# Three small re-orderings in a fused adaLN + linear attention + GEGLU kernel: one residual addition, one product's bank, two modulations

## The chip, the cores and the metric

One core of a Trainium2 chip runs the whole program. The time is device microseconds of one execution; the kernel before stands at 788.48 us, the median of three runs.

## What is computed

With x of 2048 tokens by 1024 columns, all inputs in bf16:

```
sa, ca, ga, sb, cb, gb = (silu(c) @ w_mod) cut into six rows of 1024
h = layernorm(x) * (1 + ca) + sa
x = x + ga * (linear_attention(h; wqkv, 32 heads) @ wo)
h = layernorm(x) * (1 + cb) + sb
x = x + gb * ((gelu(h @ w_gate) * (h @ w_up)) @ w_down)        # 3584 inner columns
```

## The kernel before

The tokens are 16 tiles of 128 ("chunks" c0 to c15), in four groups of 512. The work goes through four stages: layernorm and the K/Q projections; the attention sums and the output product; the feed-forward's gate and up products; the down product.

**Program order and queues.** Every instruction is recorded with `sch.op(engine, ...)` or `sch.dma(...)` together with the bytes and PSUM banks that it reads and writes. A tracker turns those into semaphore waits. Each engine (TensorE is PE, VectorE is DVE, ScalarE is ACT, GpSimd is POOL, SyncE is SP and issues nearly all transfers) then runs its list strictly in order. For the stretch from the last K tiles to the second feed-forward unit, `Sched.reorder` rewrites the lists of DVE, ACT and POOL: a planner with a cost per instruction and a due time worked back from the end picks the ready instruction that is due first. PE's and SP's lists stay as recorded.

**From attention to the feed-forward.** `wo_chunk(c)` makes 16 matmuls (L1266) of a chunk's attention output into two banks. Then one DVE instruction, `x1` (L1274), adds the result to the residual x in SBUF (`XALL`) and leaves the row sums for the next layernorm. From these come the row statistics (POOL L666 to L681, ACT L676), the normalised chunk (ACT L662) and a transposing transfer into `H2` (L705). Then the modulation by `1 + cb` and `sb` is done in place, one instruction for each of eight column blocks: on DVE (`mod2`, L726) or on ACT (`mod2_act`, L755). The chunks c2 to c13 go through a loop whose side work is written out by hand in the table `SLOT`. `pq_scale` (DVE L1258) scales the queries of a coming group by a factor that SP has loaded (`rb_load`, L1245).

**The feed-forward units.** A unit multiplies 256 columns of the gate and up weights with 512 or 1024 tokens. The 2x2 blocks of weights and inputs are multiplied in Winograd's way: seven products instead of eight, numbered 1, 2, 6, 5, 7, 3, 4 in the order in which PE makes them (`prod`, L1440). For that DVE builds sums of weights, `t_sum` into `TP` (L1416), and sums of inputs, `s_sum` into `SS` (L1396: `ss0.0` is sum 0, half 0). Products 5, 6, 7 and 3 need `SS` sums 0, 1, 2 and 3. In the very first unit the order is 1, 2, 5, 6, wo chunk 14, 7, wo chunk 15, 3, 4: the last two chunks of the attention output stand between its products. PSUM is moved along by ACT copies (L1445, L1448) and DVE additions (`padd`, L1451). Gelu is on ACT (L1463), and the product of gate and up on DVE (`y_out`, L1470). Wo chunk 15 goes into banks 0 and 1, which gelu and `y_out` of products 1 and 2 have to read first.

**The down product.** The tokens are taken in eight pairs of chunks (`d_pair`), each with four 128x512 results in four banks. The first 22 of the 28 blocks of inner columns again go through seven products (`d_prod`, L1657, 11 matmuls each), the last six blocks through plain matmuls (`down`, L1581). `DT[q][3]` holds the weight block that product 3 multiplies by. `evac` takes a finished bank: DVE multiplies it by the row `gb` (`GBB`, L1564), DVE adds x (L1565) and SP stores the result (L1566). In the last pair each result is taken out as soon as it is finished. The order there is: products 2, 6, 5, 7, result (14,0), product 4, results (15,0) and (15,1), product 3, result (14,1). Product 3 adds into the bank of result (14,1).

Of the kernel before, what the change touches and what calls it, by code (L numbers as in the profile page):

```python
# [8 lines left out]
ALU = mybir.AluOpType  # L9

P = 128
# [56 lines left out]
NJQ = (2, 2, 2, 2, 2, 1)  # L68
# [261 lines left out]
def bass_adaLN_cond__linear_attn_block__geglu_ffn__prompt_kernel(  # L330
# [18 lines left out]
    with ExitStack() as es:  # L349
# [195 lines left out]
        def pr(b):  # L545
            return [(b * 2048, (b + 1) * 2048)]
# [706 lines left out]
        def pq_scale(sg, h, gs):  # L1253
            i, t0 = sg % 2, h * HW
            for g0, g1 in gs:
# [3 lines left out]
                       rd=rng + r_rb(i, h, g0, g1), wr=rng, deps=rb_ops[sg, h], note=f"pqs{sg}.{h}.{g0}")  # L1259

        def wo_mm(c_, b0, gs):
            sg, ci = divmod(c_, CPG)
            last = [None, None]
            for g in gs:
                for half in range(2):
                    last[half] = sch.op(T, lambda e, g=g, half=half: e.matmul(  # L1266
                        PS(b0 + half), PQ[sg][:, g, ci * P:(ci + 1) * P], W2[:, g, half * 512:(half + 1) * 512],
                        start=(g == 0), stop=(g == NG - 1)),
                        rd=r_pq(sg, g, g + 1, ci * P, (ci + 1) * P) + r_w(OFF_WK, "w2", g, half * 512, (half + 1) * 512),
                        pwr=(pr(b0 + half) if g == 0 else ()), note=f"wo c{c_} g{g} h{half}")  # L1270
            if gs[-1] == NG - 1:
                for half in range(2):
                    pset_writer(b0 + half, last[half])
                sch.op(V, lambda e: e.scalar_tensor_tensor(XALL[:, c_, :], ps_all[:, b0 * 512:(b0 + 2) * 512], 1.0, XALL[:, c_, :],  # L1274
                                                           op0=ALU.mult, op1=ALU.add, accum_out=STA[:, c_, 0:1]),
                       prd=pr(b0) + pr(b0 + 1), rd=r_x(c_), wr=r_x(c_) + r_smc("st", c_, 48), note=f"x1 c{c_}")
                if c_ < 2 * CPG:
                    ln_nmean(c_)
# [101 lines left out]

        s_ops = {}

        def s_sum(p, i, j):
# [18 lines left out]
        def t_sum(u, k):  # L1402
            if k == 3:
                ap, rd = wq(u, 1, 1)
                for t in range(2):
                    sch.op(A, lambda e, t=t: e.activation(TP[3][:, t, :, :], ap[:, t, :, :], ACTF.Copy), rd=rd[t:t + 1], wr=r_tp(3, t, t + 1), note=f"brcp u{u}")
                return
            if k == 0:
                (in0, r0), (in1, r1) = wq(u, 0, 1), wq(u, 0, 0)
            elif k == 1:  # L1410
                (in0, r0), (in1, r1) = wq(u, 1, 1), (T32[0], r_tp(0))
            elif k == 2:
                (in0, r0), (in1, r1) = wq(u, 1, 1), wq(u, 0, 1)
            else:
                (in0, r0), (in1, r1) = wq(u, 1, 0), (T32[1], r_tp(1))
            sch.op(V, lambda e: e.tensor_tensor(TP[k][:], in0, in1 if k in (0, 2) else in1[:], ALU.subtract), rd=r0 + r1, wr=r_tp(k), note=f"tsum{k} u{u}")  # L1416

# [222 lines left out]

        def d_prod(ca, b0, k):
            b = b0 + {1: 0, 2: 0, 5: 3, 6: 2, 7: 2, 4: 2, 3: 1}[k]
            i = {1: None, 2: None, 5: 0, 6: 1, 7: 2, 3: 3, 4: 4}[k]
            o, n = None, nj(ca)
            for j in range(n):
# [5 lines left out]
                else:  # L1651
# [3 lines left out]
                    if i == 4:  # L1655
                        dst = dst.rearrange("p (h c) -> p h c", h=2)
                o = sch.op(T, lambda e, l_=l_, r_=r_, j=j, dst=dst: e.matmul(dst, l_[:, 0, :], r_, start=k in (1, 5) and j == 0, stop=j == n - 1, skip_group_check=True),  # L1657
                           rd=rl + rr, pwr=(pr(b) if j == 0 else ()), note=f"down P{k} c{ca} j{j}", overwrite_ok=True)
# [3 lines left out]

        later = []

        def d_first(i):
# [4 lines left out]
        def d_pair(i, hook):  # L1670
# [3 lines left out]
            parts = tuple((ca + n // 2, n % 2, b0 + n, n % 2 * 512, n % 2 * 512 + 512) for n in range(4))  # L1674
            for k in (2, 6, 5, 7, 12, 4, 14, 15, 3, 13) if last else (2, 6, 5, 7, 3, 4):
                if k > 10:
                    x = parts[k - 12]
                    down(*x, fcs, True, True)
                    evac(*x)
                    continue  # L1680
# [11 lines left out]
                elif k == 7:  # L1692
                    sch.op(V, lambda e: e.tensor_tensor(PS(b0 + 3), PS(b0 + 2), DE[:, :], ALU.add), prd=pr(b0 + 2), rd=R_DE, pwr=pr(b0 + 3), note="dpadd")
                for x in mine:
                    evac(*x)
# [27 lines left out]
        def cb1():  # L1723
# [207 lines left out]
```

## Time and profile before

| | |
|---|---|
| median of three runs | 788.48 us (788.33 to 788.61) |
| the profiled execution | 788.06 us |
| its span in the profile | 786.3 us |
| PE busy | 779.1 us, 99% |
| DVE busy | 619.5 us, 79% |
| ACT busy | 374.2 us, 48% |
| granted TensorE clock | 1.0 |

The profile is of one execution. A line of its views names an engine, a line of the kernel, `out<-in` by tile names, a shape and a count. "PEld" is the loading of matmul weights, which runs beside the matmuls. In the timeline the first two columns are the start and the length in microseconds; where several instructions are merged, the length reaches from the first start to the last end, and matmuls overlap by some 0.16 us. Brackets give the idle time of the engine before the instruction, and what ended it. 1.8 us of the execution lie outside the span.

### The profile page before, as it was taken

To read this page: it belongs to the slowest core of one execution; us is meant where nothing else is said; L and a number is where in the kernel's file an instruction comes from. 1 tells how busy PE (TensorE), PEld (TensorE's weight loads), DVE (VectorE), ACT (ScalarE), POOL (GpSimd) and SP (SyncE) were. 2 spreads that over 40 slices of the span, in tenths; PEclk is the share of its full clock that TensorE was granted. 3 is DMA by queue.
4 is the path that set the end of the run, shared out by engine and by line. 5 is a ranking of instruction groups with operands and counts; after the bars stand their busy time and mean duration, and the time that the engine had idled before them with its cause. 6 is when DMAs were issued, how large, how long until landed. Compare 5 with 4: busy or idle time off the path is not lost.

```text
span 786.3 us, 10713 instructions
## 1 busy us (share of the span) xinstructions
PE 779.1 (99%) x3890; PEld 490.5 (62%) x3890; DVE 619.5 (79%) x944; ACT 374.2 (48%) x634; POOL 48.2 (6%) x126
## 2 busy tenths in 40 slices
PE   8999999999999999999999999999999999999998
PEld 4444445666445667767676776767676466666665
DVE  6699998895789878787989889898887975555664
ACT  2497743242575487877755555465655011111011
POOL 2131300000321011100000000000000000000000
PEclk9999999999999999999999999999999999999999
DMA  9789749939998257856344764534327644433510
GB/s 288 248 172 244 163 93 245 223 76 196 208 282 218 82 149 199 240 174 202 108 135 126 242 207 146 157 108 134 117 72 252 235 162 134 135 83 123 169 53 28
DMA packets 178781, 130.24 MB, mean 166 GB/s; under 512 B 69020, under 2 KB 163492, under 8 KB 176680
## 3 DMA queue, kind: packets, MB, share of 16 engines
q1 hardware_dynamic: 178712, 129.55, 59.6%
q8 instruction: 31, 0.51, 0.3%
q14 instruction: 22, 0.18, 0.1%
q10 hardware_dynamic: 16, 0.00, 0.0%
HBM read 92.55 MB, written 23.35 MB: 147 GB/s over the span
## 4 chain that ended last, share of the span: by engine, by line
PE 93%; DVE 3%; SPq 2%; DMA 1%; issue 1%; DVEq 0%
PE ps_all L1440 44%; PE ps_all L1657 17%; PE ps_all L897 7%; PE ps_all L933 7%; PE ps_all L1581 6%; PE ps_all L882 6%; PE ps_all L1266 5%; SPq L600 1%; DMA wmq<-in_w_mod_dram 1%; DVE ss L1396 1%; DVE xall L1274 1%; SPq L605 1%; DVE pq L1258 1%; PE ps_all L915 0%; PE ps_all L1198 0%
## 5 line engine op out<-in xcount | busy, mean ns | idle before, releaser
L1440 PE MATMUL ps_all<-ss,tp 128*128 128x512 f32 x896 | 214.6, 396 | 0.4 <-DVE ss L1396 0.3
L1440 PEld LDWEIGHTS ps_all<-ss,tp 128*128 128x128 f32 x896 | 168.2, 188 | 38.8 <-DVE ss L1396 1.3
L1440 PE MATMUL ps_all<-h2a,wt 128*128 128x512 bf16 x448 | 101.6, 380 | 0.0
L1463 ACT ACTIVATE ge<-ps_all 128x512 f32<-128x512 f32 x112 | 64.1, 597 | 75.1 <-DVE ps_all L1451 61.3
L1470 DVE TENSOR_TENSOR ys<-ge,ps_all 128x512 bf16<-128x512 f32 x112 | 74.5, 684 | 6.2 <-PE ps_all L1440 3.3
L1458 DVE TENSOR_TENSOR ps_all<-ps_all,es 128x512 f32<-128x512 f32 x54 | 37.7, 700 | 50.6 <-ACT es L1448 50.2
L1657 PE MATMUL ps_all<-dt,ds 128*128 128x512 f32 x320 | 76.2, 395 | 0.0
L1440 PEld LDWEIGHTS ps_all<-h2a,wt 128*128 128x128 bf16 x448 | 38.0, 98 | 57.2 <-ACT ps_all L1445 16.9
L1416 DVE TENSOR_TENSOR tp<-wt 128x1024 fp32r<-128x1024 bf16 x56 | 68.2, 1217 | 3.2 <-issue 3.2
L1657 PEld LDWEIGHTS ps_all<-dt,ds 128*128 128x128 f32 x320 | 60.1, 188 | 13.4
L1416 DVE TENSOR_TENSOR tp<-wt,tp 128x1024 fp32r<-128x1024 bf16 x56 | 68.3, 1219 | 0.0
L882 PE MATMUL ps_all<-wk,h1T 128*128 128x512 bf16 x248 | 56.7, 379 | 0.2 <-DVE h1T L726 0.2
L933 PE MATMUL ps_all<-h1T,wq 128*128 128x512 bf16 x256 | 56.7, 379 | 0.0
L1266 PE MATMUL ps_all<-w,pq 128*128 128x512 bf16 x256 | 56.3, 379 | 0.0
L1440 PE MATMUL ps_all<-ar,tp 128*128 128x512 f32 x224 | 55.5, 390 | 0.0
L871 ACT ACTIVATE eb<-ps_all 128x512 f32<-128x512 f32 x64 | 36.4, 593 | 37.4 <-PE ps_all L882 14.4
L1440 PEld LDWEIGHTS ps_all<-ar,tp 128*128 128x128 f32 x224 | 42.0, 188 | 8.9
L1668 ACT ACTIVATE ps_all<-ps_all 128x512 f32<-128x512 f32 x8 | 4.7, 582 | 87.4 <-PE ps_all L1657 87.4
L1445 ACT ACTIVATE ps_all<-ps_all 128x512 f32<-128x512 f32 x56 | 32.6, 582 | 28.2 <-PE ps_all L1440 28.2
L1581 PE MATMUL ps_all<-wd,yb 128*128 128x512 bf16 x192 | 44.3, 380 | 0.0
L933 PEld LDWEIGHTS ps_all<-h1T,wq 128*128 128x128 bf16 x256 | 25.0, 98 | 30.0
L1266 PEld LDWEIGHTS ps_all<-w,pq 128*128 128x128 bf16 x256 | 24.7, 98 | 29.9 <-ACT w L1200 0.3
(144 smaller groups left out, 1012.8 us busy)
## 6 DMA issues: line engine op xcount, KB each, us to landing
wt<-in_B_w_gate_dram SPq DMA_DIRECT2D x28, 512.0 KB, 4.1
wt<-in_B_w_up_dram SPq DMA_DIRECT2D x28, 512.0 KB, 5.3
scr_y<-ys SPq DMA_DIRECT2D x28, 512.0 KB, 2.9
ya<-scr_y SPq DMA_DIRECT2D x8, 1408.0 KB, 6.5
rb<-scr_rd SPq DMA_DIRECT2D x32, 256.0 KB, 6.4
wmst<-in_w_mod_dram SPq DMA_DIRECT2D x6, 1024.0 KB, 5.8
wd<-in_B_w_down_dram SPq DMA_DIRECT2D x6, 1024.0 KB, 7.4
wmq<-in_w_mod_dram SPq DMA_DIRECT2D x8, 512.0 KB, 6.8
```

What stands on the lines that cost most here:

```text
L871: sch.op(A, lambda e: e.activation(EB[i][:, :], PS(bank), ACTF.Exp), prd=pr(bank), wr=rng, note=f"{note}.exp")
L882: o = sch.op(T, lambda e, dc=dc: e.matmul(PS(bank), H1[sg][:, ci, dc, :], W_[:, dc, jg * 512:(jg + 1) * 512], start=(dc == 0), stop=(dc == ...
L897: o = sch.op(T, lambda e, c_=c_: e.matmul(PS(bank, 0, n), PK[c_][:, g * P:(g + 1) * P], xrow(c_, o_, o_ + n), start=(c_ == 0), stop=(c_ == ...
L933: o = sch.op(T, lambda e, dc=dc: e.matmul(PS(b), WQ[:, dc, qc * P:(qc + 1) * P], H1[sg][:, :, dc, :], start=(dc == 0), stop=(dc == NDC - 1 ...
L1266: last[half] = sch.op(T, lambda e, g=g, half=half: e.matmul(PS(b0 + half), PQ[sg][:, g, ci * P:(ci + 1) * P], W2[:, g, half * 512:(half + ...
L1416: sch.op(V, lambda e: e.tensor_tensor(TP[k][:], in0, in1 if k in (0, 2) else in1[:], ALU.subtract), rd=r0 + r1, wr=r_tp(k), note=f"tsum{k} ...
L1440: o = sch.op(T, lambda e, l_=l_, r_=r_, dc=dc: e.matmul(PS(b), l_, r_, start=fresh and dc == 0, stop=dc == ND2 - 1, skip_group_check=True) ...
L1458: sch.op(V, lambda e: e.tensor_tensor(PS(BC + t), PS(BC + t), ES[t][:, :], ALU.add), prd=pr(BC + t), rd=r_2k(OFF_ES[t], f"es{t}"), pwr=pr( ...
L1463: sch.op(A, lambda e: e.activation(GE[i][:, :], PS(b), ACTF.Gelu_apprx_tanh), prd=pr(b), wr=r_2k(OFF_GE[i], f"ge{i}"), note="gelu")
L1470: sch.op(V, lambda e: e.tensor_tensor(YS[s_][:, 2 * h:2 * h + 2, t, :], q(GE[i][:, :]), q(PS(b + 1)), ALU.mult), rd=r_2k(OFF_GE[i], f"ge{i ...
L1581: o = sch.op(T, lambda e, fc=fc, q=q, m=m: e.matmul(PS(b, 0, n), y_at(c_, fc), WDT[q][:, m, c0:c1], start=False, stop=last and fc == fcs[- ...
L1657: o = sch.op(T, lambda e, l_=l_, r_=r_, j=j, dst=dst: e.matmul(dst, l_[:, 0, :], r_, start=k in (1, 5) and j == 0, stop=j == n - 1, skip_g ...
```

## The change

Three edits, in two places of the program.

1. *Residual addition of c7.* The weight sum `t_sum(0, 0)` moves from slot 6 to slot 7 of the table and has to wait for `x1 c7`. On DVE, `x1 c7` now stands ahead of that sum instead of behind it. Also `ss0.1` is recorded one slot earlier, and `x1 c13` has to wait for it: the two change places.
2. *Two modulations to ACT.* Of the four DVE modulations of `H2`'s second half (c6 and c7, column blocks 0 to 3), blocks 0 and 1 go to ACT, behind the 12 that it does there already.
3. *The last pair of the down product.* Result (14,1) and product 3 change places on PE, and product 3 gets a bank of its own, bank 0, with a fresh start. The six `DT[q][3]` are multiplied by `gb` in place, on DVE (`t_gb`: three after product 6, three after product 7), so that product 3 comes out already multiplied. While product 3 runs, the rest of result (14,1) is multiplied by `gb` into `DE` and x is added (`evac_part`); behind product 3 one DVE addition is left (`evac_sum`), and then the store.

The lists that come out of the planner differ from those before on PE, DVE and ACT in these places alone; POOL and SP keep their order.

```diff
-                sch.op(V, lambda e: e.scalar_tensor_tensor(XALL[:, c_, :], ps_all[...], 1.0, XALL[:, c_, :],
+                x1_ops[c_] = sch.op(V, lambda e: e.scalar_tensor_tensor(XALL[:, c_, :], ps_all[...], 1.0, XALL[:, c_, :],
...
-                       prd=pr(b0) + pr(b0 + 1), rd=r_x(c_), wr=r_x(c_) + r_smc("st", c_, 48), note=f"x1 c{c_}")
+                       prd=pr(b0) + pr(b0 + 1), rd=r_x(c_), wr=r_x(c_) + r_smc("st", c_, 48),
+                       deps=[s_ops[0, 0, 1]] if c_ == 13 else [], note=f"x1 c{c_}")
...  (t_sum)
+                   deps=[x1_ops[7]] if u == 0 and k == 0 else [], note=f"tsum{k} u{u}")
...
+        def t_gb(q):
+            n = NJQ[q]
+            t_, r_ = dt_ap(q, 3, 0, n)
+            sch.op(V, lambda e: e.tensor_tensor(t_, t_.bitcast(f32), GBB[:, 512:1024].unsqueeze(1).to_broadcast([P, n, 512]), ALU.mult), rd=r_ + R_GBB, wr=r_, ...)
...  (d_prod: bank `own` where given, and start=True on its first matmul)
+        def evac_part(c_, k, b, c0, c1):
+            X_ = XD[c_ // 2 % 2][:, c_ % 2, c0:c1]
+            sch.op(V, lambda e: e.tensor_tensor(DE[:, :], PS(b), GBB[:, c0:c1], ALU.mult), prd=pr(b), rd=R_GBB, wr=R_DE, ...)
+            sch.op(V, lambda e: e.tensor_tensor(DE[:, :], DE[:, :], X_, ALU.add), rd=r_xd(c_, c0, c1) + R_DE, wr=R_DE, ...)
+        def evac_sum(c_, k, b, c0, c1):
+            X_ = XD[c_ // 2 % 2][:, c_ % 2, c0:c1]
+            sch.op(V, lambda e: e.tensor_tensor(X_, PS(b), DE[:, :], ALU.add), prd=pr(b), rd=R_DE, wr=r_xd(c_, c0, c1), ...)
+            sch.dma(Q, lambda e: e.dma_start(out_v[:, c_, c0:c1], X_), rd=r_xd(c_, c0, c1), ...)
...  (d_pair)
-            for k in (2, 6, 5, 7, 12, 4, 14, 15, 3, 13) if last else (2, 6, 5, 7, 3, 4):
+            for k in (2, 6, 5, 7, 12, 4, 14, 15, 13, 3) if last else (2, 6, 5, 7, 3, 4):
+                if last and k == 3:
+                    d_prod(ca, b0, 3, 0)
+                    evac_sum(*parts[1][:2], 0, *parts[1][3:])
+                    continue
...
+                if last and k in (6, 7):
+                    for q in range(3):
+                        t_gb(q if k == 6 else q + 3)
...  (SLOT)
-                6: lambda: (mod2(0, 0, 2), t_sum(0, 0), x_dma(10, 12)),
-                7: lambda: (t_sum(0, 1), mod2(0, 2, 2), x_dma(12, 14)),
+                6: lambda: (mod2(0, 0, 2), x_dma(10, 12)),
+                7: lambda: (t_sum(0, 0), t_sum(0, 1), mod2(0, 2, 2), x_dma(12, 14)),
...
-                12: lambda: (s_sum(0, 0, 0), mod2(1, 2, 2, 0, ND2)),
-                13: lambda: (s_sum(0, 0, 1), s_sum(0, 1, 0), s_sum(0, 1, 1), pq_scale(3, 1, GH[0] + GH[1]), s_sum(0, 2, 0))}
+                12: lambda: (s_sum(0, 0, 0), mod2_act(1, 2, 2, 0, 2), mod2(1, 2, 2, 2, ND2), s_sum(0, 0, 1)),
+                13: lambda: (s_sum(0, 1, 0), s_sum(0, 1, 1), pq_scale(3, 1, GH[0] + GH[1]), s_sum(0, 2, 0))}
```

More of the change, by code (lines that the diff above doesn't have):

```diff
@@ L1259, in pq_scale @@
                        rd=rng + r_rb(i, h, g0, g1), wr=rng, deps=rb_ops[sg, h], note=f"pqs{sg}.{h}.{g0}")
+        x1_ops, s_ops = {}, {}
         def wo_mm(c_, b0, gs):
@@ L1639, in d_s, with d_prod @@
                 sch.op(V, lambda e, dst=dst, in0=in0, in1=in1, op=op: e.tensor_tensor(dst, in0, in1, op), rd=r0 + r1, wr=wr, note=f"dssum{i} {cb}")
-        def d_prod(ca, b0, k):
-            b = b0 + {1: 0, 2: 0, 5: 3, 6: 2, 7: 2, 4: 2, 3: 1}[k]
+        def t_gb(q):
+            n = NJQ[q]
+            t_, r_ = dt_ap(q, 3, 0, n)
+            sch.op(V, lambda e: e.tensor_tensor(t_, t_.bitcast(f32), GBB[:, 512:1024].unsqueeze(1).to_broadcast([P, n, 512]), ALU.mult), rd=r_ + R_GBB, wr=r_,
+                   note=f"{'dtsum' if n == 2 else 'dtone'} gb{q}")
+        def d_prod(ca, b0, k, own=None):
+            b = b0 + {1: 0, 2: 0, 5: 3, 6: 2, 7: 2, 4: 2, 3: 1}[k] if own is None else own
             i = {1: None, 2: None, 5: 0, 6: 1, 7: 2, 3: 3, 4: 4}[k]
@@ L1656, in d_prod @@
                         dst = dst.rearrange("p (h c) -> p h c", h=2)
-                o = sch.op(T, lambda e, l_=l_, r_=r_, j=j, dst=dst: e.matmul(dst, l_[:, 0, :], r_, start=k in (1, 5) and j == 0, stop=j == n - 1, skip_group_check=True),
+                o = sch.op(T, lambda e, l_=l_, r_=r_, j=j, dst=dst: e.matmul(dst, l_[:, 0, :], r_, start=(k in (1, 5) or own is not None) and j == 0, stop=j == n - 1, skip_group_check=True),
                            rd=rl + rr, pwr=(pr(b) if j == 0 else ()), note=f"down P{k} c{ca} j{j}", overwrite_ok=True)
```

14 lines of the change are left out of this document (10 added, 4 removed).

## Prediction

> **What bounds the kernel now.** I read the page first: busy shares, clock, chain.
>
> ```profile
> PE 779.1 (99%) x3890; PEld 490.5 (62%) x3890; DVE 619.5 (79%) x944; ACT 374.2 (48%) x634; POOL 48.2 (6%) x126
> ...
> PEclk9999999999999999999999999999999999999999
> ...
> PE 93%; DVE 3%; SPq 2%; DMA 1%; issue 1%; DVEq 0%
> ```
>
> PE is busy in 99% of the span at a clock row full of nines, and 93% of the chain is matmuls. So a gain can only come where PE waits, or behind its last matmul. The view of waits, for PE alone, has four rows. Three are of lines of the first two stages, the largest of them here; the fourth is one that the change reaches:
>
> ```profile
> PE ps_all L630 <- POOL bmask L583: 2.1, 1, 2.1
> ...
> PE ps_all L1440 <- DVE ss L1396: 0.3, 1, 0.3
> ```
>
> It is a wait of the first feed-forward unit for an input sum (L1396). Nothing behind that unit is listed. PE's timeline there (start, length) shows more than that row:
>
> ```profile
> 217.67 24.55 PE L1266 MATMUL ps_all<-w,pq 128*128 128x512 bf16 x113
> ...
> 245.32 4.40 PE L1440 MATMUL ps_all<-ss,tp 128*128 128x512 f32 x16
> 249.56 3.63 PE L1266 MATMUL ps_all<-w,pq 128*128 128x512 bf16 x16
> 253.48 2.11 PE L1440 MATMUL ps_all<-ss,tp 128*128 128x512 f32 x8 [0.29 <-DVE ss L1396]
> 255.43 3.63 PE L1266 MATMUL ps_all<-w,pq 128*128 128x512 bf16 x16
> 258.70 2.19 PE L1440 MATMUL ps_all<-ss,tp 128*128 128x512 f32 x8
> 260.73 1.52 PE L1440 MATMUL ps_all<-ar,tp 128*128 128x512 f32 x6
> ```
>
> Two stalls stand in these starts. (a) Products 5 and 6 are 16 fp32 matmuls, from 245.32 to 249.56: 4.24 us. Two runs of fp32 matmuls of the tail price them:
>
> ```profile
> 778.33 2.89 PE L1657 MATMUL ps_all<-dt,ds 128*128 128x512 f32 x11
> 781.07 1.47 PE L1581 MATMUL ps_all<-wd,yb 128*128 128x512 bf16 x6
> ```
>
> 11 of them last from 778.33 to 781.07, 2.74 us. By 8 from 258.70 to 260.73 (2.03) and these 11, one costs 0.23 and the change of kind in front some 0.2. So 16 should take 3.9: product 6 stalls 0.34. (b) Wo chunk 14 and product 7 take 255.43 - 249.56 = 5.87; the same kinds and counts, chunk 15 and product 3, take 260.73 - 255.43 = 5.30. Product 7 stalls 0.57. Together 0.91 us, all of it owed to DVE:
>
> ```profile
> 219.41 2.15 DVE L726 TENSOR_SCALAR h2a<-h2a,cb1T,sbT 128x256 bf16<-128x256 bf16 x8
> 224.71 1.23 DVE L1416 TENSOR_TENSOR tp<-wt 128x1024 fp32r<-128x1024 bf16 x1 [3.15 <-issue]
> 225.85 1.22 DVE L1274 SCALAR_TENSOR_TENSOR xall<-ps_all,xall 128x1024 bf16<-128x1024 f32 x1
> ...
> 231.38 2.49 DVE L1258 TENSOR_TENSOR pq<-pq,rb 128x512 bf16<-128x512 bf16 x4
> ...
> 239.50 1.21 DVE L1274 SCALAR_TENSOR_TENSOR xall<-ps_all,xall 128x1024 bf16<-128x1024 f32 x1
> ...
> 241.78 1.10 DVE L726 TENSOR_SCALAR h2b<-h2b,cb1T,sbT 128x256 bf16<-128x256 bf16 x4
> ...
> 245.19 2.36 DVE L1396 TENSOR_TENSOR ss<-ss,h2a 128x1024 fp32r<-128x1024 f32 x2
> ...
> 252.21 1.22 DVE L1396 TENSOR_TENSOR ss<-h2a,h2b 128x1024 fp32r<-128x1024 bf16 x1
> 253.34 1.22 DVE L1274 SCALAR_TENSOR_TENSOR xall<-ps_all,xall 128x1024 bf16<-128x1024 f32 x1
> ...
> 254.49 0.68 DVE L1470 TENSOR_TENSOR ys<-ge,ps_all 128x512 bf16<-128x512 f32 x1
> 255.08 2.35 DVE L1396 TENSOR_TENSOR ss<-h2a,ss 128x1024 fp32r<-128x1024 bf16 x2
> ```
>
> `ss1.1` ends at 245.19 + 2.36 = 247.55, just before product 6; the last half of sum 2 ends at 252.21 + 1.22 = 253.43, just before product 7. DVE runs without a pause from 224.71 on, and ahead of that it stands idle for 3.15 us, for a weight transfer that `tsum0` needs, with `x1 c7` (225.85) queued behind. The kernel's end is the other place:
>
> ```profile
> 762.36 0.70 DVE L1564 TENSOR_TENSOR ps_all<-ps_all,gbb 128x512 f32<-128x512 f32 x1 [2.10 <-PE ps_all L1581]
> ...
> 768.64 0.96 DVE L1639 TENSOR_TENSOR ds<-ya,ds 128x768 fp32r<-128x768 bf16 x1 [4.85 <-PE ps_all L1657]
> ...
> 772.26 0.70 DVE L1693 TENSOR_TENSOR ps_all<-ps_all,de 128x512 f32<-128x512 f32 x1 [1.06 <-PE ps_all L1657]
> 773.58 0.70 DVE L1564 TENSOR_TENSOR ps_all<-ps_all,gbb 128x512 f32<-128x512 f32 x1 [0.61 <-PE ps_all L1581]
> 774.38 0.69 DVE L1565 TENSOR_TENSOR xd<-ps_all,xd 128x512 bf16<-128x512 f32 x1
> 777.43 0.70 DVE L1564 TENSOR_TENSOR ps_all<-ps_all,gbb 128x512 f32<-128x512 f32 x1 [2.36 <-PE ps_all L1581]
> ...
> 782.58 0.70 DVE L1564 TENSOR_TENSOR ps_all<-ps_all,gbb 128x512 f32<-128x512 f32 x1 [2.39 <-PE ps_all L1581]
> 783.31 0.69 DVE L1565 TENSOR_TENSOR xd<-ps_all,xd 128x512 bf16<-128x512 f32 x1
> ```
>
> After PE's last matmul (781.07 + 1.47 = 782.54) come a multiplication and an addition, then store and close, 2.3 us from 784.00 to the span's end.
>
> **`x1 c7` first.** PE's row at 217.67 ends at 242.22 with chunk 13; a bf16 matmul follows the one before after 0.216 (16 last 3.63, with some 0.39 for one alone), a chunk takes 3.45, and six chunks earlier c7 is finished: 242.22 - 20.7 = 221.5. The modulations end at 219.41 + 2.15 = 221.56. So `x1 c7` fits into the idle time (until 222.7), and `tsum0` still starts with its weights at 224.71. Everything behind `x1 c7` moves up by 1.14 (225.85 less 224.71, one place). Two covers could fail. The query scaling at 231.38 would start at 230.24 and needs its transfers:
>
> ```profile
> L1245 SPq DMA_DIRECT2D rb<-scr_rd x4: 412/421/523, 222.9 to 224.5; - x4
> ...
> DMA to landing us min/median/max: 3.9/4.6/5.3
> ```
>
> The last issue is at 224.5, and at most 5.3 later it has landed: 229.8, before 230.24. And `x1 c12` (239.50) needs chunk 12: 242.22 - 3.45 = 238.76, with release and a second wait 238.87. DVE would be ready for it at 239.50 - 1.14 = 238.36, so only 239.50 - 238.87 = 0.63 goes on.
>
> **Two modulations to ACT.** DVE's four (241.78 to the addition at 242.80) cost 0.255 each, so two save 0.51. ACT gets two more:
>
> ```profile
> 233.67 6.01 ACT L755 ACTIVATE h2b<-h2b,sbT,cb1T 128x256 bf16<-128x256 bf16 x12 [0.47 <-DMA h2b<-xl]
> 243.12 0.58 ACT L1445 ACTIVATE ps_all<-ps_all 128x512 f32<-128x512 f32 x1 [3.44 <-PE ps_all L1440]
> ```
>
> Its 12 take 0.50 each, and 14 end at 233.67 + 7.0 = 240.7. DVE asks for them (`ss0.1`) at about 241.8, and ACT's next work, 243.12, came after 3.44 us idle: hidden, with 1.1 us to spare. If that cover were gone, `ss0.1` would wait for ACT. The Trainium skill, ScalarE: Activation LUTs, "Rules for kernel authors", speaks against this edit: multiplications and additions belong on VectorE, which it says is up to about three times faster in bf16. The rows agree in direction, 0.50 against 0.255; by that rule alone the edit would lose 2 x 0.245 = 0.49, by the rows of who waits for whom it gains DVE 0.51.
>
> **The swap of `ss0.1` and `x1 c13`** moves no work. It adds two same-engine waits, for which some 0.08 each is my estimate by the tail's rows: multiplication to addition is 0.73 (782.58, 783.31), and 0.80 where the addition also waits for its x transfer (773.58, 774.38). Queued behind both are all later DVE rows here. Sum for DVE at `ss1.1` and later: 0.63 + 0.51 - 0.16 = 0.98.
>
> **What PE gets of it.** Product 6's sum ends at 247.55 - 0.98 = 246.57, and PE needs it at 247.1 (245.32 + 0.2 + 7 x 0.23): the 0.34 goes. The last matmul of chunk 14 then starts at 249.56 + 15 x 0.216 - 0.34 = 252.46. With it PE wants the weights of product 7, whose sum ends at 253.43 - 0.98 = 252.45; PE saw such an end after 0.05 (253.43, 253.48), so at 252.50: 0.03 is left of the 0.57. Late next is chunk 15. It must wait for `y_out` (254.49), which stands on DVE behind `x1 c14` (253.34), and that now waits for PE's chunk 14 itself: end 253.19 - 0.34 = 252.85, release 0.04 as at 782.54, two more waits some 0.1, start 252.99. `y_out` follows 1.15 later (253.34, 254.49), at 254.14, and ends at 254.82. Chunk 15's second matmul waits for it with its weight load:
>
> ```profile
> L1266 PEld LDWEIGHTS ps_all<-w,pq 128*128 128x128 bf16 x256 | 24.7, 98 | 29.9 <-ACT w L1200 0.3
> ```
>
> PE would have come to this load at 255.43 - 0.91 + 0.03 = 254.55 and now does at 254.87. Of the 0.32 it makes good 0.12, since a load takes 0.098 of a matmul's 0.216. So a new stall of 0.2 takes the place of the old one (bounds 0, if the release is quicker, and 0.4). Sum 3 (255.08, ending 257.4) is needed at 258.7 and moves up with the rest. The feed-forward behind it has no wait of PE in the list above, and its transfers are issued by what PE and DVE finish, so the gain is kept: 0.91 - 0.03 - 0.2 = 0.68.
>
> **The tail.** The last six plain matmuls and product 3's 11 change places at equal sum. Behind the last matmul one DVE instruction of 0.69 is left instead of two: 783.31 - 782.58 = 0.73 less. The addition waits for PE and for DVE, one wait more than the multiplication had: -0.07 by the rows at 773.58, with bounds 0 and 0.12. Nearly 0.67. Cover for what is added: `t_gb` multiplies 128x1024 in fp32, both operands in SBUF, which the trace does not have. The nearest row has one such operand:
>
> ```profile
> L1396 DVE TENSOR_TENSOR ss<-ss,h2a 128x1024 fp32r<-128x1024 f32 x2 | 2.4, 1222 | 0.0
> ```
>
> I take its 1.22 (spacing 1.14), and twice that, 2.4, as the outer bound for two; less would change nothing. The first three take 3.5 and lie in DVE's idle time before 762.36 (2.10) and 768.64 (4.85); they push one extraction, which nothing on PE awaits, to 765.2. The next three (two and a half in size) run from 772.96 to about 776.0, push the extraction at 773.58 to 777.4, and the one at 777.43 hardly moves. The plain part of result (14,1) is finished at 780.0 (778.33, six matmuls and a release) and DVE at 780.2; multiplying and adding end at 781.6, 1.0 before product 3 does. Stores keep their order on SP.
>
> **Sum.** 0.68 + 0.67 = 1.35 us. Against the profiled execution: 788.06 - 1.35 = 786.71; the median of the runs is 0.42 above that execution, so 788.48 - 1.35 = 787.1.
>
> **Rivals.** *Both halves in full*: chunk 15 is not held, and the last addition's second wait costs nothing: 0.91 + 0.73 = 1.64, 786.8. For it: the 0.2 hangs on 0.3 us of release times. Against: DVE's order is fixed, and `y_out` stands behind `x1 c14`.
>
> *Only one half arrives*: DVE's 0.98 is lost to a later end. The nearest is ACT: if its 14 modulations end 2 us later than 240.7, `ss0.1` gives up 0.9 and products 6 and 7 stall as before. Then the tail's 0.67 alone is left, 787.8; with the front alone it is the same. For it: ACT starts these when a transfer lands (0.47 idle at 233.67). Against: the 1.1 to spare. This is the case in which the Trainium skill's rule on VectorE, cited above, would decide.
>
> *It does not do what it says*: PE's first unit stays as it was, and DVE's last addition ends where it did: 788.5.
>
> *Slower*: `t_gb` at 2.4 each. The second batch lasts from 772.96 to 779.0, the three extractions behind it (0.73 + 0.69 each) to 783.2, multiplying and adding for (14,1) to 784.6, the last addition to 785.3, against 784.00 now: 1.3 lost, 0.68 gained in front, 789.1. The tail's gain begins to shrink at a batch of 4.1 us (772.96 + 4.1 + 4.2 + 1.4 = 782.6), and from 5.4 on the whole is slower; 3.0 is expected. For it: the operation is not in the trace. Against: the row at 1222 with an fp32 input is no dearer than those with bf16 (1.23 at 224.71). The Trainium skill, VectorE: DVE Perf Modes, "Rules for kernel authors", advises a small count of chained DVE instructions. The seven more that stand here count against the change by it; the idle times in the rows above (2.10, 4.85, 2.36) say that they are hidden.
>
> **How the numbers follow.** A measurement of this kernel can tell about 0.2%, 1.58 us, from no change. Chances: forecast 0.52, both in full 0.20, one half 0.17, no effect 0.04, slower 0.07. The forecast's own bounds (chunk 15 held 0 to 0.4, second wait 0 to 0.12) give 1.10 to 1.60, 786.9 to 787.4. The range takes in both in full (with 0.2 for the spread of runs, 786.6) and one half (787.9); the last two cases, 0.11, are left out. Faster by over 0.2% needs a time under 786.9: four fifths of the second case and a sixth of the forecast, 0.25. Slower by over 0.2% is 790.1: the slow rival at a still higher price, and what I have overlooked, 0.05. The rest, 0.70, lies within.
>
> **What would show it.** Right: `x1 c7` at about 221.6; `x1 c12` behind a PE wait near 238.9; the runs of products 5 and 6 in 3.9 us; sum 2's last half ending near 252.45; chunk 15 starting near 254.5 and its second matmul late; one DVE instruction behind the last matmul, starting within 0.1 of it. Wrong: a DVE idle time with a transfer or ACT as its end between 226 and 246; PE waiting for L1258 or L1396 as before; `t_gb` rows of over 1.6 us; or the last addition starting later than PE's last matmul by more than 0.15.

## The result, and the profile after

The changed kernel takes 786.56 us (median of 13 runs, 786.20 to 787.25), the kernel before on the same chip 788.41 (13 runs, 787.87 to 789.48): a ratio of 0.9976, 95% interval 0.9968 to 0.9985. That is 1.85 us (1.2 to 2.5 by the interval), where 1.35 were forecast; the median lies 0.04 us under the range, and in the class "faster by over 0.2%", which had a chance of 0.25. The profiled execution takes 786.35 us, its span is 784.6.

The page of the changed kernel: busy time, clock and chain.

```profile
PE 774.4 (99%) x3832; PEld 490.2 (62%) x3890; DVE 625.8 (80%) x949; ACT 375.0 (48%) x636; POOL 47.1 (6%) x126
...
PEclk9999999999999999999999999999999999999999
...
PE 71%; DVE 1%; issue 0%; DVEq 0%
```

PE stays the bound at full clock; DVE has six microseconds more work. The chain of this profile can be followed back only to 219.35 us, through 72% of the span, so its 71% for PE can't be set beside the 93% before. PE's view of waits in the changed kernel (microseconds in total, times, longest):

```profile
PE ps_all L630 <- POOL bmask L583: 2.1, 1, 2.1
PE ps_all L882 <- DMA wk<-in_A_wqkv_dram: 0.5, 1, 0.5
PE ps_all L768 <- DMA wmq<-in_w_mod_dram: 0.3, 1, 0.3
PE ps_all L882 <- DVE h1T L726: 0.2, 1, 0.2
```

The wait for an input sum, L1440 for L1396 before, is gone; the four that are left belong to the first 200 us, which no edit touches. PE's timeline at the first feed-forward unit of the changed kernel (start, length; with the edits, line 1440 has become 1442 and 1266 has become 1268):

```profile
245.11 4.03 PE L1442 MATMUL ps_all<-ss,tp 128*128 128x512 f32 x16
248.98 3.63 PE L1268 MATMUL ps_all<-w,pq 128*128 128x512 bf16 x16
252.38 2.11 PE L1442 MATMUL ps_all<-ss,tp 128*128 128x512 f32 x8
254.63 3.41 PE L1268 MATMUL ps_all<-w,pq 128*128 128x512 bf16 x15
257.69 2.20 PE L1442 MATMUL ps_all<-ss,tp 128*128 128x512 f32 x8
259.73 1.99 PE L1442 MATMUL ps_all<-ar,tp 128*128 128x512 f32 x8
```

From product 5 to product 4, the last row, it now takes 259.73 - 245.11 = 14.62 us, before 260.73 - 245.32 = 15.41. The weight loads show where the waits went, since the trace has all 3890 of them in each kernel. Before:

```profile
247.60 1.69 PEld L1440 LDWEIGHTS ps_all<-ss,tp 128*128 128x128 f32 x8 [0.51 <-DVE ss L1396]
...
253.48 1.68 PEld L1440 LDWEIGHTS ps_all<-ss,tp 128*128 128x128 f32 x8 [0.78 <-DVE ss L1396]
```

After the change:

```profile
245.09 3.63 PEld L1442 LDWEIGHTS ps_all<-ss,tp 128*128 128x128 f32 x16
...
252.37 1.68 PEld L1442 LDWEIGHTS ps_all<-ss,tp 128*128 128x128 f32 x8 [0.26 <-DVE ss L1397]
254.33 0.10 PEld L1268 LDWEIGHTS ps_all<-w,pq 128*128 128x128 bf16 x1 [0.27 <-issue]
254.63 1.41 PEld L1268 LDWEIGHTS ps_all<-w,pq 128*128 128x128 bf16 x8 [0.20 <-DVE ys L1472]
```

Products 5 and 6 are one unbroken row of 16 loads; the load of product 7 idles 0.26 instead of 0.78; and one small wait is new, chunk 15's second load for the first y product, as forecast. DVE in the changed kernel:

```profile
221.50 1.21 DVE L1276 SCALAR_TENSOR_TENSOR xall<-ps_all,xall 128x1024 bf16<-128x1024 f32 x1
...
224.79 1.23 DVE L1417 TENSOR_TENSOR tp<-wt 128x1024 fp32r<-128x1024 bf16 x1 [2.08 <-DMA wt<-in_B_w_up_dram]
...
230.58 2.50 DVE L1258 TENSOR_TENSOR pq<-pq,rb 128x512 bf16<-128x512 bf16 x4
...
237.56 1.22 DVE L1276 SCALAR_TENSOR_TENSOR xall<-ps_all,xall 128x1024 bf16<-128x1024 f32 x1
238.70 1.22 DVE L1276 SCALAR_TENSOR_TENSOR xall<-ps_all,xall 128x1024 bf16<-128x1024 f32 x1
...
239.84 1.22 DVE L1397 TENSOR_TENSOR ss<-h2b 128x1024 fp32r<-128x1024 bf16 x1
240.98 0.60 DVE L726 TENSOR_SCALAR h2b<-h2b,cb1T,sbT 128x256 bf16<-128x256 bf16 x2
241.68 1.22 DVE L1397 TENSOR_TENSOR ss<-h2b 128x1024 fp32r<-128x1024 bf16 x1
...
244.09 2.36 DVE L1397 TENSOR_TENSOR ss<-ss,h2a 128x1024 fp32r<-128x1024 f32 x2
...
251.11 1.21 DVE L1397 TENSOR_TENSOR ss<-h2a,h2b 128x1024 fp32r<-128x1024 bf16 x1
252.74 1.22 DVE L1276 SCALAR_TENSOR_TENSOR xall<-ps_all,xall 128x1024 bf16<-128x1024 f32 x1 [0.42 <-PE ps_all L1268]
...
253.89 0.68 DVE L1472 TENSOR_TENSOR ys<-ge,ps_all 128x512 bf16<-128x512 f32 x1
```

`x1 c7` stands at 221.50 in the wait for the weights, and the first weight sum still starts when they have landed, at 224.79. `x1 c12` (238.70) follows `x1 c11` (237.56) after 1.14 us, the pace of these additions: in this profile it doesn't wait for PE. ScalarE has 14 modulations now and is idle after them:

```profile
233.64 6.99 ACT L755 ACTIVATE h2b<-h2b,sbT,cb1T 128x256 bf16<-128x256 bf16 x14 [2.97 <-DMA h2b<-xl]
242.91 0.58 ACT L1447 ACTIVATE ps_all<-ps_all 128x512 f32<-128x512 f32 x1 [2.29 <-PE ps_all L1442]
```

And the tail, DVE and PE of the changed kernel:

```profile
759.19 3.49 DVE L1646 TENSOR_TENSOR dt<-dt,gbb 128x1024 fp32r<-128x1024 f32 x3
...
771.89 2.95 DVE L1646 TENSOR_TENSOR dt<-dt,gbb 128x1024 fp32r<-128x1024 f32 x3
...
776.45 0.70 DVE L1566 TENSOR_TENSOR ps_all<-ps_all,gbb 128x512 f32<-128x512 f32 x1 [0.20 <-PE ps_all L1583]
...
781.61 0.69 DVE L1680 TENSOR_TENSOR xd<-ps_all,de 128x512 bf16<-128x512 f32 x1 [1.09 <-PE ps_all L1665]
774.94 4.06 PE L1583 MATMUL ps_all<-wd,yb 128*128 128x512 bf16 x18
778.65 2.86 PE L1665 MATMUL ps_all<-dt,ds 128*128 128x512 f32 x11
```

The last matmul ends at 781.51, the one DVE instruction behind it starts at 781.61.

Since the loads are complete, their starts divide each span: up to the 401st load (the start), from the 1501st to the 2001st (the front, with the first unit in it), and from the 3801st to the end of the span (the tail). The stretch from the 2001st to the 3801st takes 402.07 us in every kernel, and that from the 401st to the 1501st 184.85 to 184.91 in all but one. Between the two profiles the start gave 62.05 - 61.85 = 0.21, the front 112.97 - 112.19 = 0.77 and the tail 24.32 - 23.60 = 0.72; together 1.70, the difference of the spans (each taken before rounding). 1.49 of it lies in the two stretches that the edits touch.

### The profile page after: what moved, and what is told of

It is laid out like the page before. It is cut to its first block, busy times and chain, and to the rows that moved or that the text cites. A ratio compares the mean times of both kernels' runs of the same rounds, so it can differ in the third digit from the quotient of the medians.

```text
span 784.6 us, 10665 instructions
## 1 busy us (share of the span) xinstructions
PE 774.4 (99%) x3832; PEld 490.2 (62%) x3890; DVE 625.8 (80%) x949; ACT 375.0 (48%) x636; POOL 47.1 (6%) x126
## 4 chain that ended last, share of the span: by engine, by line
PE 71%; DVE 1%; issue 0%; DVEq 0%
PE ps_all L1442 44%; PE ps_all L1665 17%; PE ps_all L1583 6%; PE ps_all L1268 4%; DVE h2a L726 0%; DVE xall L1276 0%; DVE xd L1680 0%; DVE ys L1472 0%; DVEq L1914 0%
## 5 line engine op out<-in xcount | busy, mean ns | idle before, releaser
L1442 PE MATMUL ps_all<-h2a,wt 128*128 128x512 bf16 x421 | 95.6, 379 | 1.8
L1583 PE MATMUL ps_all<-wd,yb 128*128 128x512 bf16 x185 | 42.6, 379 | 0.5
```

Of the source, the lines that this page charges most:

```text
L1442: o = sch.op(T, lambda e, l_=l_, r_=r_, dc=dc: e.matmul(PS(b), l_, r_, start=fresh and dc == 0, stop=dc == ND2 - 1, skip_group_check=True) ...
L1583: o = sch.op(T, lambda e, fc=fc, q=q, m=m: e.matmul(PS(b, 0, n), y_at(c_, fc), WDT[q][:, m, c0:c1], start=False, stop=last and fc == fcs[- ...
```

## The experiments

**Each half alone.** `e1_front` has the change without its tail, `e2_tail` the kernel before with the tail of the change:

```diff
...
-            for k in (2, 6, 5, 7, 12, 4, 14, 15, 3, 13) if last else (2, 6, 5, 7, 3, 4):
+            for k in (2, 6, 5, 7, 12, 4, 14, 15, 13, 3) if last else (2, 6, 5, 7, 3, 4):
...
+                if last and k in (6, 7):
+                    for q in range(3):
+                        t_gb(q if k == 6 else q + 3)
...
```

> The two edits in front alone: x1 c7 ahead of the first weight sum with the swap of ss0.1 and x1 c13, and two H2 modulations on ScalarE; the last pair stays as it was. Theory of the prediction, with the new stall at chunk 15 as predicted: 0.68 us less than before, ratio 0.9991. Reading of the changed kernel's profile, where PE runs 0.77 earlier from the second feed-forward unit on once its earlier start is taken out: 0.77 less, ratio 0.9990. Rival, a third gain in the program's start or elsewhere that goes with these edits: 1.1 us or more. If the halves do not arrive: no change.

> The edit of the last pair alone: product 3 in a bank of its own with weights multiplied by gb; the front stays as it was. Theory of the prediction: 0.67 less than before; reading of the changed kernel's profile: 0.69; ratio 0.9991 by both. Rival, a third gain that goes with this edit (the store or the close after it becoming shorter): 1.0 us or more.

Measured on one chip with the kernel before at 788.42 (33 runs): the front alone 787.34, ratio 0.9986 (0.9978 to 0.9995); the tail alone 787.61, 0.9991 (0.9983 to 1.0). These are 1.08 and 0.81 us, above what was expected of each (0.68 to 0.77, and 0.67 to 0.69), but their intervals reach from 0.4 to 1.7 and from 0 to 1.3. By the loads the front is 112.19 in the first and the tail 23.59 in the second, each as in the whole change. So, by the loads, the halves don't touch each other and add up.

**The same two kernels again.** The change once more, and the kernel before against itself.

> The changed kernel once more, in the same series as its two parts and a copy of the kernel before. If the two parts are all there is, 1.35 us (prediction) to 1.47 us (profile) less than before, and the sum of the two parts run alone; ratio 0.9981 to 0.9983. If there is a third gain, 1.85 less again (ratio 0.9976), and more than the parts' sum by some 0.4. Its profile tells by the start of PE's second projection stage how much of the difference lies in the program's first 60 us, which no edit touches.

> The kernel before, unchanged, as a kernel of this series. Its difference to the kernel before is what runs of one program differ by: 0 is expected, with up to 0.5 us between medians if the program's start varies as much as between the two profiles at hand (0.21 us). A ratio clearly off 1 would say that the 1.85 contained something that is not the change.

The change: 786.76 (786.28 to 787.32), ratio 0.9981 (0.9972 to 0.9989), 1.66 us. The kernel before: 788.93, 1.0007 (0.9998 to 1.0016): half a microsecond between two medians of one kernel. The times carry the sum of the change, not its parts; those are read from the profiles. And the profiles held a surprise: the fronts of `e4_before_again` and `e2_tail`, which are the front of the kernel before, took 113.22 and 113.20, not 112.97. PE of `e4_before_again`:

```profile
245.36 2.12 PE L1440 MATMUL ps_all<-ss,tp 128*128 128x512 f32 x8
247.75 2.11 PE L1440 MATMUL ps_all<-ss,tp 128*128 128x512 f32 x8 [0.27 <-DVE ss L1396]
```

Product 6 waits here 0.2 longer than in the profile of the forecast. The chain of waits of `e2_tail` tells what it hangs on (start, length, what):

```profile
212.46 3.17 SPq L705
215.73 2.46 SPq L705
218.24 4.62 DMA wt<-in_B_w_gate_dram
...
227.03 1.14 DVE tp L1416
```

Two transposes on SP, behind them the weight transfers of the first unit, behind their landing the first weight sum, and from there DVE without a pause. In the profile of the forecast SP had those two transposes done in 5.50 us, in `e4_before_again` in 5.90.

**One edit of the front at a time.** `e5_c7_only` puts only tile 7's addition ahead of the first weight sum; `e6_act_only` gives only the two modulations to ScalarE.

```diff
e5:
...
+                   deps=[x1_ops[7]] if u == 0 and k == 0 else [], note=f"tsum{k} u{u}")
...
-                6: lambda: (mod2(0, 0, 2), t_sum(0, 0), x_dma(10, 12)),
-                7: lambda: (t_sum(0, 1), mod2(0, 2, 2), x_dma(12, 14)),
+                6: lambda: (mod2(0, 0, 2), x_dma(10, 12)),
+                7: lambda: (t_sum(0, 0), t_sum(0, 1), mod2(0, 2, 2), x_dma(12, 14)),
e6:
-                12: lambda: (s_sum(0, 0, 0), mod2(1, 2, 2, 0, ND2)),
+                12: lambda: (s_sum(0, 0, 0), mod2_act(1, 2, 2, 0, 2), mod2(1, 2, 2, 2, ND2)),
```

> Of the whole change only this is done: tile 7's residual addition stands ahead of the first weight sum on DVE; the four H2 modulations stay on DVE, their order against tile 13's addition is that of the kernel before, and the tail is that of the kernel before. Theory (DVE's lateness is set by the landing of the first unit's weights, and the addition now fits into the wait for them): DVE runs 0.6 us earlier from tile 12's addition on, which then meets the matmuls; product 6 no longer waits (0.37 to 0.57 us in the profiles without the edits), product 7 waits 0.3 to 0.5; the kernel takes 0.6 us less than the kernel before, 787.8. Rival (the addition's place alone frees DVE by its whole 1.14 us): neither product waits, 1.0 us less, 787.4. Rival (the weights land when they land and everything behind them keeps its place): no change, both waits stay.

> Of the whole change only this is done: two of the four H2 modulations ahead of the second feed-forward sums go to ScalarE; all else is the kernel before. Theory (each stall of the first unit is owed to DVE's lateness, and every 0.5 us taken from DVE ahead of both counts): DVE is 0.5 us earlier at the second half of sum 1; of the 0.9 to 1.1 us that products 6 and 7 wait together 0.5 is gone, the rest waits at one of them; the kernel takes 0.5 us less, 787.9. Rival (ScalarE returns the two modulations late, and DVE waits for them): no gain, DVE idle ahead of the first half of sum 1, and both products still wait.

Measured 787.71, ratio 0.9992 (0.9984 to 1.0001), and 787.96, 0.9996 (0.9987 to 1.0005), with the kernel before at 788.48: 0.77 and 0.52 us less, each too small for its interval to exclude no change. The loads are clearer: the front takes 112.45 and 112.46. In both, product 6 doesn't wait, and product 7 waits 0.40. Either edit alone frees product 6 and leaves product 7 waiting as long as the other does. Only the whole front frees product 7, and that has the swap of `ss0.1` and `x1 c13` besides the two edits. In `e5_c7_only` DVE met PE at two places, not one:

```profile
238.70 1.22 DVE L1276 SCALAR_TENSOR_TENSOR xall<-ps_all,xall 128x1024 bf16<-128x1024 f32 x1
...
240.99 1.11 DVE L726 TENSOR_SCALAR h2b<-h2b,cb1T,sbT 128x256 bf16<-128x256 bf16 x4
242.08 1.22 DVE L1276 SCALAR_TENSOR_TENSOR xall<-ps_all,xall 128x1024 bf16<-128x1024 f32 x1
```

`x1 c12` starts 1.25 after the addition before it (at 237.45, not shown) and 6.45 us ahead of PE's product 5 (245.15), the very distance that the forecast put there (245.32 - 238.87). `x1 c13` follows the four modulations by 1.09 instead of 1.02 (241.78 to 242.80 before) and starts 0.20 after PE has left chunk 13 for the unit's first product (241.88). It does so in `e6_act_only` (242.27 and 242.07) and in the next run too (242.15 and 241.95): chunk 13 holds it in all three.

**The weights earlier, everything else as before.**

```diff
-                3: lambda: pq_scale(1, 1, GH[0] + GH[1]),
-                4: lambda: (cb1(), wt_dma(0)),
+                3: lambda: (pq_scale(1, 1, GH[0] + GH[1]), wt_dma(0)),
+                4: lambda: cb1(),
```

> The kernel before with one thing moved: SP issues the first unit's two weight transfers one transpose earlier. Theory (the first weight sum starts when these transfers land, and the product waits follow from that): the sum starts 1 us or more earlier than 224.7, DVE gains 0.6 us until tile 12's addition meets the matmuls, product 6 waits no more, product 7 0.3 to 0.5, and the kernel takes 0.6 us less, 787.8, as much as with tile 7's addition put ahead. Rival (the weights are not what the sum waits for, or the transpose that is now later holds DVE up by as much): no change or slower, product 6 still waits 0.37 to 0.57.

787.64 us, ratio 0.9991 (0.9982 to 1.0), 0.84 less; the front takes 112.43, product 7 waits 0.40, product 6 not at all. SP and DVE of this run:

```profile
216.16 0.58 SPq L1352 DMA_DIRECT2D wt<-in_B_w_gate_dram x1
216.78 1.99 SPq L1352 DMA_DIRECT2D wt<-in_B_w_up_dram x1
...
223.60 1.23 DVE L1416 TENSOR_TENSOR tp<-wt 128x1024 fp32r<-128x1024 bf16 x1 [1.57 <-issue]
```

Counted from the 401st load, the transfers start 2.0 us earlier and the sum 1.0 us earlier (161.66 instead of 162.66). Without an edit on DVE the same stalls go as with tile 7's addition put ahead. That settles what made DVE late: the landing.

**The landing against the wait, and the change with early weights.** Two further profiles of the kernel before, and the edit of the last run laid over the whole change.

> The kernel before, one more look. Theory (product 6's wait follows the landing of the first unit's weights): measured from the start of the matmul stream, a first weight sum that starts 0.1 us later goes with a wait that is 0.1 us longer; with the pairs so far (162.66 us and 0.37, 162.84 and 0.56, 162.89 and 0.58) a wait of 0.3 to 0.7. Rival (the profile of the forecast was an outlier for another reason): 0.56 to 0.58 wherever the sum starts.

> As the look before it, for one more pair: by the theory the wait of product 6 is the start of the first weight sum, counted from the start of the matmul stream, less 162.3 us, within 0.05; by the rival 0.56 to 0.58 whatever that start.

> The whole change, and besides the first unit's two weight transfers issued one transpose earlier. Theory (with the edits DVE is held by the matmuls ahead of tile 12's addition, no more by the landing): the first weight sum starts about 1 us earlier and DVE loses that again in front of tile 12's addition; the products keep their spacing, no change against the changed kernel, 786.6. Rival (the landing still sets DVE's pace, and the two gains add up): the sums come 0.5 us or more earlier, but since products 6 and 7 no longer wait, at most the 0.1 us of chunk 15 is gained, 786.5. Rival (the transpose that is now later holds DVE up): product 6 or 7 waits again, 0.2 us or more slower.

For all kernels with the front of before, from the starts of the loads and of DVE's first weight sum (product 6's wait is the time from the 1501st to the 1511th load over the 2.29 that it takes in each kernel without one):

| profile | first weight sum, us after the 401st load | product 6 waits | product 7 waits | front |
|---|---|---|---|---|
| `e12_before_look` | 162.63 | 0.33 | 0.59 | 113.01 |
| `e11_before_look` | 162.65 | 0.34 | 0.54 | 112.93 |
| before, of the forecast | 162.66 | 0.37 | 0.56 | 112.97 |
| `e4_before_again` | 162.84 | 0.56 | 0.57 | 113.22 |
| `e2_tail` | 162.89 | 0.58 | 0.57 | 113.20 |

The wait of product 6 is the start of the first weight sum less 162.3, within 0.03; the rival, 0.56 to 0.58 everywhere, is out. The kernels with the whole front of the change saw the sum start at 161.65 to 163.05, and their fronts all took 112.17 to 112.21. `e9_change_early_weights` is the earliest of them: 786.61 us, ratio 0.9979 (0.997 to 0.9988), no better than the change. Its DVE:

```profile
224.15 1.23 DVE L1417 TENSOR_TENSOR tp<-wt 128x1024 fp32r<-128x1024 bf16 x1 [0.55 <-DMA wt<-in_B_w_up_dram]
...
231.09 2.50 DVE L1258 TENSOR_TENSOR pq<-pq,rb 128x512 bf16<-128x512 bf16 x4 [1.25 <-DMA rb<-scr_rd]
...
239.38 1.23 DVE L1276 SCALAR_TENSOR_TENSOR xall<-ps_all,xall 128x1024 bf16<-128x1024 f32 x1
```

What the earlier weights gave was lost again, but not where it was expected: DVE idles 1.25 us for the query scaling's own transfer, and only some 0.2 go to the wait ahead of `x1 c12`, which stands 6.45 ahead of product 5 (245.83) as in the other kernels that PE holds there.

**The y product first.** The whole change, with the order of tile 14's addition and the first y product turned round:

```diff
...
-                       deps=[s_ops[0, 0, 1]] if c_ == 13 else [], note=f"x1 c{c_}")
+                       deps={13: lambda: [s_ops[0, 0, 1]], 14: lambda: [y_op[0]]}.get(c_, list)(), note=f"x1 c{c_}")
...
-        ORD0 = (1, 2, 5, 6, lambda: (s_sum(0, 2, 1), gelu(BA)), (14, BE),
-                lambda: (y_out(0, BA, 0, 0, 0), s_sum(0, 3, 0), s_sum(0, 3, 1)), 7, (15, BA), 3, 4)
+        ORD0 = (1, 2, 5, 6, lambda: (s_sum(0, 2, 1), gelu(BA), y_out(0, BA, 0, 0, 0)), (14, BE),
+                lambda: (s_sum(0, 3, 0), s_sum(0, 3, 1)), 7, (15, BA), 3, 4)
```

> The whole change, and besides the first y product ahead of tile 14's addition on DVE. Theory (chunk 15's first matmul of its second half waits 0.1 us for that y product, the one stall that the change makes): that wait goes, the kernel takes 0.1 us less than the changed kernel, 786.5. Rival (the y product waits for the GELU, and tile 14's addition behind it comes late for the bank that it frees): product 7 or chunk 15 starts 0.2 to 0.5 us later, the kernel 0.2 to 0.5 us slower than the changed kernel, 787.0. It is read from the spacing of the products in the profile, since 0.1 us lies under what the times can tell.

786.38 us, ratio 0.9977 (0.9968 to 0.9986), 2.10 less: the fastest of all, though 0.18 from the change is under what times can tell. By the loads chunk 15 no longer waits (0.09 to 0.13 in the other kernels with the front's edits), product 7 waits 0.08, and the front takes 112.09, 0.1 less. The y product pays a wait for the GELU, and PE doesn't notice:

```profile
253.06 0.69 DVE L1472 TENSOR_TENSOR ys<-ge,ps_all 128x512 bf16<-128x512 f32 x1 [0.66 <-ACT ge L1465]
253.78 1.22 DVE L1276 SCALAR_TENSOR_TENSOR xall<-ps_all,xall 128x1024 bf16<-128x1024 f32 x1
```

**The gating twice.**

```diff
                     for q in range(3):
                         t_gb(q if k == 6 else q + 3)
+                        t_gb(q if k == 6 else q + 3)
```

> The whole change, with each of the six gating multiplications of the third product's weight sums done twice; that product's contribution is thereby multiplied by the gate's row twice. Theory of the forecast (the second batch, 3.0 us, lies beside matmuls; what it delays costs nothing up to 4.1 us and 1 to 1 from there): a batch of 5.9 to 6.4 us ends the kernel 1.8 to 2.3 us later than the changed kernel, 788.4 to 788.9, tail 25.4 to 25.9 instead of 23.6. Rival (the batch's delay reaches the last evacuation only through tile 14's two, and the matmuls that follow cover more than 4.1 us): 0 to 0.5 us later. Rival (already the first batch of 3.5 us was not free, twice it delays the products that its evacuations feed): over 3 us later.

788.42 us, ratio to the kernel before 1.0005 (0.9996 to 1.0014), 1.81 above `e9_change_early_weights` on the same chip. The tail takes 25.51 instead of 23.60, 1.91 more; the front stays at 112.17. DVE:

```profile
759.25 7.26 DVE L1646 TENSOR_TENSOR dt<-dt,gbb 128x1024 fp32r<-128x1024 f32 x6
...
771.94 6.20 DVE L1646 TENSOR_TENSOR dt<-dt,gbb 128x1024 fp32r<-128x1024 f32 x6
778.06 0.69 DVE L1566 TENSOR_TENSOR ps_all<-ps_all,gbb 128x512 f32<-128x512 f32 x1
...
783.57 0.69 DVE L1680 TENSOR_TENSOR xd<-ps_all,de 128x512 bf16<-128x512 f32 x1
```

From 771.94 to the last addition DVE has no pause, and that addition follows its own engine, not PE. The first batch at twice its length, 7.26 us, still fitted into the idle time behind it.

## Why the prediction was right or wrong

The mechanism was right in most parts, with one wait that did not show (at `x1 c12`), and the sum was too small, because one execution's stalls were taken for the kernel's own: 1.35 forecast, 1.49 between the two profiles in the parts that the edits touch, and 1.85 by the medians.

- **What bounds the kernel**: right. The two stalls, read from starts as 0.34 and 0.57, are 0.37 and 0.56 by the loads.
- **`x1 c7`**: its start is right to 0.1 us (221.6 forecast, 221.50). The cut from 1.14 to 0.63 is right in size, but in this profile not in cause: `x1 c12` stands 6.41 ahead of product 5, before 5.82, so 0.59 arrived, and no wait for PE stands in front of it. What was lost is 0.29 by the weights, which were used that much later against PE (162.95 and 162.66 after the 401st load), and 0.26 on DVE from there to `x1 c12` (238.70 - 224.79 = 13.91, where 239.50 - 224.71 - 1.14 = 13.65 would have been had). Most of this, 0.19, lies at the query scaling (230.58, where 229.25 + 1.14 = 230.39 was open to it), for which the forecast's cover failed: it let the last of the four transfers land 5.3 after its issue, from a row that holds the landings of three, and the trace has the fourth land at 230.46, 6.05 after its issue at 224.41. The nearness of 0.59 to 0.63 is luck of this execution. The wait for chunk 12 itself is real: in six other kernels (`e1_front`, `e3_both_again`, `e5_c7_only`, `e7_early_weights`, `e9_change_early_weights`, `e10_gate_twice`) `x1 c12` stands 6.45 ahead of product 5.
- **ScalarE**: right. Its 14 modulations end at 240.63 (240.7 forecast), and DVE asks for them at 241.68. The rule that the Trainium skill states in ScalarE: Activation LUTs, "Rules for kernel authors" (multiplications and additions on VectorE), fits the price of one instruction, 0.50 us against 0.255; it does not decide here: with this edit alone the front is 0.5 us shorter, where by the rule it would have been 0.49 longer, since ScalarE stood idle and PE was waiting for DVE.
- **The swap of `ss0.1` and `x1 c13`**: undervalued. The forecast saw no work moved and two waits of 0.08. The waits cost 0.21: from `ss0.0` to `ss1.0` it is 244.09 - 239.84 = 4.25, before 245.19 - 240.64 = 4.55, and 0.51 of modulations left. But in the three kernels that keep the old order, chunk 13 holds `x1 c13` until 0.20 after the first product begins. With both edits in the old order that would be 242.05 (241.85 + 0.20) where DVE is free at 241.6, and `ss1.0` would start near 244.5 rather than 244.09. By `e5_c7_only`, where it starts at 244.49, product 7 would then still wait some 0.4. So the swap, which the forecast booked as a loss of 0.16, would be needed for product 7's gain. This is worked out from the rows; the change without the swap was not run.
- **DVE's sum**: 0.98 forecast for the end of `ss1.1`, 247.55 - 246.45 - 0.21 of the start = 0.89. It made no difference, as PE needed it only at 246.9 of this profile.
- **Left over at product 7**: 0.03 forecast, 0.03 in this profile, 0.00 and 0.01 in the others.
- **Chunk 15**: the mechanism was right, the size too large. `y_out` ended at 253.89 + 0.68 = 254.57 (254.82 less the start's 0.21 is 254.61), but PE lost 0.09 here and 0.12 to 0.13 in the repetitions, not 0.2. Of its wait, 254.57 + 0.05 for the release less the 254.34 at which it would have come (254.55 less 0.21), 0.28, it made good 0.19, where the forecast allowed it 0.12.
- **The tail**: 0.72 instead of 0.67. The second wait of the last addition cost what was forecast: it starts 0.10 behind the last matmul, before 0.04. Too small was "at equal sum": PE's last 29 matmuls now take 781.51 - 774.94 = 6.57, before 782.54 - 775.92 = 6.62, and the one thing that differs there is the order: the 18 plain ones stand together, with one change of kind fewer. The gating's price (3.49 and 2.95 us for the two batches; 3.5 and 3.0 forecast) and the point from which it would cost were right: a second batch of 6.12 to the next row's start, 2.0 over the 4.1 of the forecast, ended 1.91 late. The slower rival was sound in its mechanism and had the wrong price in it. The sentence of the Trainium skill in VectorE: DVE Perf Modes, "Rules for kernel authors", that asks for few chained instructions, is borne out by this run alone, where the idle time was used up; in the change itself the added instructions cost nothing.
- **The step that failed: the sum against one profiled execution.** The forecast took its 0.91 of stalls, and the 0.42 between that execution and the median, for the kernel's own. Neither is fixed. Product 6's wait follows the landing of two transfers and was 0.33 to 0.37 in three profiles and 0.56 to 0.58 in two, while the forecast put 0.34, at the low end; and the change removes whichever it is: the front of the five takes 113.07 on average, that of the change 112.19, so the front's term is 0.88 (0.74 to 1.03 by profile) where 0.68 stood. With the tail it makes 1.60.

  The start varies from 61.68 to 62.51 in all these profiles, and gave the two that were compared 0.21 by chance; and the changed kernel's median lies 0.21 above its profiled execution, not 0.42. So of the miss of 0.57 at the median (787.13 - 786.56) 0.14 is in the terms (chunk 15 and tail), 0.21 in the start, and 0.21 in the offset. The offset is no property of the kernel either: from the profiled execution to the median it is -0.46 (`e9_change_early_weights`) to 0.58 us (`e4_before_again`) in the kernels here. The range's low end took the whole of both halves and 0.2 for all such spread, which was too little. How much of the 1.85 is the change itself stays open by some tenths: the medians gave 1.66 when it was run again, 1.47 with early weights (786.61 against 788.08) and 2.10 with the y product first, and the loads 1.60. The 0.04 by which the median lies under the range tell little: two medians of the kernel before lie 0.51 apart, and the repetition's, 786.76, lies inside.
- **The rivals**: *both in full* (786.8) is nearest in time, but not in mechanism: chunk 15 is held and the second wait is paid. *One half* did not happen to the whole change; the halves alone gave 787.34 and 787.61, where 787.8 was forecast. Of the signs of being right, the wait for PE ahead of `x1 c12` is missing in this profile; of the signs of being wrong, DVE's idle time for a transfer between 226 and 246 is there, but small: 0.11 us ahead of the query scaling, too short for the views to list.

## What to carry to other kernels

When a stall goes back to a transfer that landed some microseconds earlier, the stall in one profile is one draw: here its size moved one for one with the landing (over 0.26 us), and an edit that gives the engine slack removes the draw with it, so the gain is as uncertain as the stall was. Before moving work into an engine's idle time, find the next place where that engine meets the bound (here two additions held by their matmuls, and a scaling held by its transfer): it caps what the move can give, and two edits ahead of the same cap do not add. Times alone don't resolve edits of half a microsecond here; counting the complete weight loads does, to some 0.02 us.

## What was not expected of the hardware

A transfer that is issued at a fixed place in a queue does not land at a fixed time here: in the five profiles of the kernel before's front, on PE's clock (from the 401st load), SP issued the second weight transfer at 156.87 to 157.27 us, since the transposes ahead of it take 5.50 to 5.90, and the first weight sum followed 5.49 to 5.80 us later; the two together put it 0.26 us apart. The first 60 us vary more, by 0.82 us (61.68 to 62.51 up to the 401st load), in kernels that are the same up to there; PE's view of waits names a mask, the transfer of the conditioning input and weight transfers in changing shares, and which of them decides was not tried. Behind that, 402.07 us of the feed-forward come out alike to the hundredth in every kernel. Only `e10_gate_twice` took 0.23 more between the 401st and the 1501st load, which no edit touches; its tail is read from its own loads, and the cause is open.
